# First loads, warmup and first attention step of a fused attention and gated-MLP kernel, re-ordered

## The chip, the cores and the metric

The kernel runs on one core of one Trainium2 chip. The metric is device time in microseconds (us), lower is better; each version is run several times and the median is quoted. "Faster" or "slower" needs a difference of 2%.

Engines are named PE (TensorE matmul), PEld (its weight loads), DVE (VectorE), ACT (ScalarE), POOL (GpSimd) and SP (SyncE); a "q" behind a name is that engine's instruction queue, where DMAs (memory transfers) are issued. "L133" is line 133 of the kernel in question; the same line of code has other numbers in other versions.

## The reference, cut to what matters

```python
x = A_x                                   # 1 x 2048 x 448, bf16
xn = _layernorm(x)
# A: 16 heads of 28, each query sees the 256 keys up to itself
q, k, v = split(xn @ wqkv)
p = softmax(where(0 <= i - j < 256, q k^T * 28**-0.5, -1e9))
A = (p @ v) @ wo
# B: gated MLP, hidden size 1792
B = (gelu(xn @ w_gate) * (xn @ w_up)) @ w_down
return x + A + B
```

x is cut into 16 tiles of 128 rows, the queries into four blocks of four tiles. The change concerns only what comes before and in the first step: loads of x and of the q, k, v weights, layer norm of tiles 0 to 7, their transposes, v of tiles 0 to 3, q and k of the first head group, and the first score groups. Below, this stretch of some 20 us is called the head.

## The kernel before

The loads. `wv` is the v part of the weights, `wraw` the q and k part; both queues, SP's and ACT's, share the same 16 DMA engines.

```python
nc.sync.dma_start(out=x_sb[:, 0, :], in_=xv[:, 0, :])
nc.scalar.dma_start(out=x_sb[:, 1, :], in_=xv[:, 1, :])
nc.sync.dma_start(out=x_sb[:, 2:4, :], in_=xv[:, 2:4, :])
nc.sync.dma_start(out=wv[:, 0:3, :], in_=rows(A_wqkv, 0, 3)[:, :, 2 * D:3 * D])
nc.scalar.dma_start(out=wraw[:, 0:3, :], in_=rows(A_wqkv, 0, 3)[:, :, 0:2 * D])
# ... the last 64 rows of wv and wraw, two small loads each
nc.sync.dma_start(out=x_sb[:, 4:8, :], in_=xv[:, 4:8, :])
# ... later x_sb[:, 8:16, :]
```

The first step. `stat` is a tile's mean and variance on DVE, `rstd` turns them into 1/sigma on ACT (the row of operations called `lnv` and `rstd_all`), `norm` writes the normalised tile `xn` in a wide and a narrow piece, `transp` transposes it on PE (`tp`) and copies it to `xnT`, `pads` spreads q,k columns into 32-wide heads (`wqp`, `wkp`), `gen_v` and `gen_qk` are the v, q and k products (`pv`, `pq`, `pk`).

```python
warmup(10)                     # matmuls on zeros, only to raise PE's clock
stat(0); rstd(0, 1); stat(1); rstd(1, 1)
norm(0); transp(0, 1, nc.scalar.copy, "o")
norm(1); warmup(1); transp(1, 1, nc.scalar.copy, "d")
stat(2); stat(3); rstd(2, 2)
# ... pads of the first head group, w3p (the last 64 rows of q and k)
norm(2); norm(3)
run(gen_v(0, (0,)))            # v of tiles 0, 1
qk = gen_qk(0, (0,), 0, 2 * P); next(qk)
transp(2, 1, nc.scalar.copy, "o"); transp(3, 1, nc.vector.tensor_copy, "m")
stat(4)
run(qk)                        # q, k of the first group, first half
stat(5)
pads(nc.vector.tensor_copy, wqp, slice(1, 4)); pads(nc.vector.tensor_copy, wkp, slice(1, 4))
run(gen_qk(0, (0,), 2 * P, 2 * P))   # second half
rstd(4, 2)
stat(6)
v23 = gen_v(0, (2,)); next(v23); next(v23)   # v of tiles 2, 3, ahead of the scores
norm(4); norm(5); stat(7)
```

## Time and profile before

The kernel before took 227.83 us (227.75 to 228.38, 3 runs).

| what, profiled execution of before | us |
|---|---|
| first matmul of v (`pv`) | 7.51 |
| first exp (`p_sb`) starts | 14.11 |
| fourth score group (`sc`) starts | 20.40 |
| first load of the gelu table on ACT | 39.45 |
| second load of the gelu table | 89.53 |
| last residual addition starts | 221.31 |
| span end | 226.5 |

The last four rows are landmarks: the two table loads stand at the end of the first and of the second query block. The profile's span is some 1.7 us shorter than the device time.

From the DMA issues of the first 13 us of the kernel before (what, queue, count, size, us from issue to landing):

```profile
x_sb<-in_A_x_dram SPq DMA_DIRECT2D x1, 448.0 KB, 4.5
...
x_sb<-in_A_x_dram SPq DMA_DIRECT2D x1, 224.0 KB, 3.6
```

The first line is x tiles 4 to 7: issued at 4.78, so landed at about 9.3. The second is x tiles 2 and 3: issued at 1.26, landed at about 4.86. And from the DMA view of the kernel before, 4 to 5 us only (total; then the ScalarE queue q10: packets, MB, share of the 16 engines' time):

```profile
DMA packets 255, 0.40 MB, mean 401 GB/s; under 512 B 15, under 2 KB 255, under 8 KB 255
...
q10 hardware_dynamic: 207, 0.37, 95.7%
```

Here, between 4 and 5 us, the early loads run at 401 GB/s, in packets of 1.8 KB (0.37 MB by 207).

### The profile page before, as it was taken

The numbers are of one execution on the slowest core, as the hardware profiler recorded it, in microseconds if no ns is written. First come the engines' busy times: TensorE is split into PE (matmuls) and PEld (weight loads), VectorE is DVE, ScalarE is ACT, GpSimd is POOL, SyncE is SP. The second block draws the span as 40 slices with busy tenths as digits, with TensorE's granted clock in tenths as the row PEclk, the third lists the DMA queues.
The fourth block names the chain that finished last, engine by engine and source line by source line (L and its number), as shares of the span: only waits on it lengthen the run. The fifth ranks groups of instructions, "written<-read, shape, count | busy, mean of one in ns | idle before, by whom it ended". The sixth has DMA issues, their size and how long they took to land.

```text
span 226.5 us, 5405 instructions
## 1 busy us (share of the span) xinstructions
PE 215.8 (95%) x2237; PEld 97.2 (43%) x2262; DVE 147.5 (65%) x353; ACT 133.2 (59%) x129; POOL 43.2 (19%) x63
## 2 busy tenths in 40 slices
PE   6989999999999999999999999999999999999990
PEld 2533333344444444444444445444344435334570
DVE  5896887778675637588655666596355776679310
ACT  4578897524878876423768886333576776763000
POOL 8514767320000002222000002222000002222000
PEclk9999999999999999999999999999999999999998
DMA  6914999111100100001300100000000000100011
GB/s 215 332 24 74 322 320 303 60 23 37 37 0 24 25 5 22 26 0 28 68 0 23 25 4 25 23 0 0 0 4 20 25 5 5 42 3 0 22 42 29
DMA packets 17990, 12.69 MB, mean 56 GB/s; under 512 B 9704, under 2 KB 16936, under 8 KB 17960
## 3 DMA queue, kind: packets, MB, share of 16 engines
q1 hardware_dynamic: 17416, 11.48, 18.3%
q10 hardware_dynamic: 544, 0.80, 1.0%
q8 instruction: 19, 0.31, 0.6%
q14 instruction: 11, 0.09, 0.1%
HBM read 8.77 MB, written 1.84 MB: 47 GB/s over the span
## 4 chain that ended last, share of the span: by engine, by line
PE 79%; DVE 6%; DMA 3%; SPq 3%; ACT 3%; POOL 2%; issue 2%; DVEq 0%
PE po L301 16%; PE gt L218 15%; PE u L218 11%; PE po L296 5%; PE sc L539 5%; PE gt L223 5%; PE ov L501 4%; PE ue L218 4%; PE pq L218 3%; PE pk L218 3%; PE pv L218 3%; DMA wraw<-in_A_wqkv_dram 2%; POOL oN L451 2%; PE pq L223 2%; DMA oc<-ri 1%
## 5 line engine op out<-in xcount | busy, mean ns | idle before, releaser
L543 ACT ACTIVATE p_sb<-sc 128x2048 bf16<-128x2048 f32 (+2 forms) x42 | 73.9, 1759 | 10.2 <-PE sc L539 8.5
L301 PE MATMUL po<-wd,hT 128*128 128x448 bf16 (+1 forms) x238 | 50.0, 342 | 0.0
L376 ACT ACTIVATE ge<-gt 128x1024 bf16<-128x1024 f32 x28 | 28.7, 1024 | 35.3 <-PE u L223 22.1
L218 PE MATMUL gt<-xnT,wg 128*128 128x512 bf16 x162 | 39.3, 380 | 1.2 <-issue 0.8
L451 POOL TENSOR_TENSOR oN<-oc,rb 128x512 bf16<-128x512 f32 x10 | 12.7, 1269 | 118.6 <-DVE rb L489 50.1
L380 DVE TENSOR_TENSOR hT<-ge,u 128x512 bf16<-128x512 bf16 x42 | 26.9, 682 | 11.7 <-ACT ge L376 11.5
L218 PE MATMUL u<-xnT,wu 128*128 128x512 bf16 x120 | 30.2, 379 | 0.3
L301 PEld LDWEIGHTS <-hT 128*128 128x128 bf16 x238 | 21.6, 98 | 18.6 <-issue 2.2
L432 DVE TENSOR_TENSOR p_sb<-p_sb,masks 128x256 bf16<-128x256 bf16 (+1 forms) x90 | 24.6, 328 | 0.0
L218 PEld LDWEIGHTS <-wg 128*128 128x128 bf16 x168 | 15.1, 98 | 22.1 <-issue 6.0
L218 PEld LDWEIGHTS <-wu 128*128 128x128 bf16 x168 | 16.0, 98 | 19.2 <-issue 1.0
L507 DVE TENSOR_TENSOR oc<-oc,ov 128x512 f32<-128x512 f32 x12 | 8.2, 687 | 19.4 <-ACT oc L506 19.4
L539 PE MATMUL sc<-qT,kT 32*64 32x320 bf16 (+7 forms) x640 | 16.9, 263 | 0.5 <-ACT p_sb L543 0.3
L442 POOL TENSOR_SCALAR_AFFINE_SELECT p_sb<-p_sb 128x512 bf16<-128x512 bf16 (+1 forms) x20 | 14.3, 732 | 13.2 <-ACT p_sb L543 13.2
L306 DVE TENSOR_TENSOR res<-po,x_sb 128x448 bf16<-128x448 f32 (+1 forms) x17 | 9.9, 585 | 10.3 <-PE po L301 9.9
L296 PE MATMUL po<-wo,oN 128*128 128x448 bf16 (+1 forms) x68 | 16.3, 343 | 0.0
L506 ACT COPY oc<-ov 128x512 f32<-128x512 f32 x12 | 7.0, 585 | 15.8 <-POOL oN L451 13.4
L267 DVE CAST kT<-pk 128x512 bf16<-128x512 f32 (+1 forms) x17 | 11.0, 649 | 7.9 <-PE pk L223 7.9
L451 POOL TENSOR_TENSOR oN<-oc,l 128x512 bf16<-128x512 f32 x6 | 8.4, 1394 | 30.6 <-DVE l L468 30.6
L335 DVE CAST hT<-ue 128x512 bf16<-128x512 f32 x14 | 9.0, 686 | 7.1 <-PE ue L223 7.1
L223 PE MATMUL gt<-xnT,wgu 64*128 64x512 bf16 x49 | 13.6, 380 | 0.1
L266 ACT CAST qT<-pq 128x512 bf16<-128x512 f32 (+1 forms) x17 | 9.5, 558 | 6.5 <-PE pk L223 6.5
(75 smaller groups left out, 239.9 us busy)
## 6 DMA issues: line engine op xcount, KB each, us to landing
out_dram<-res SPq DMA_DIRECT2D x15, 112.0 KB, 1.8
wd<-in_B_w_down_dram SPq DMA_DIRECT2D x1, 1568.0 KB, 12.6
wu<-in_B_w_up_dram SPq DMA_DIRECT2D x1, 1344.0 KB
wg<-in_B_w_gate_dram SPq DMA_DIRECT2D x1, 1344.0 KB, 10.7
x_sb<-in_A_x_dram SPq DMA_DIRECT2D x1, 896.0 KB, 5.7
wraw<-in_A_wqkv_dram ACTq DMA_DIRECT2D x1, 672.0 KB, 4.9
x_sb<-in_A_x_dram SPq DMA_DIRECT2D x1, 448.0 KB, 4.5
wo<-in_A_wo_dram SPq DMA_DIRECT2D x4, 98.0 KB
```

What stands on the lines that cost most here:

```text
L218: nc.tensor.matmul(ps, lhsT=lhs(c), rhs=rhs(c), start=start and c == 0, stop=stop and c == 2, skip_group_check=True)
L223: nc.tensor.matmul(ps, lhsT=lhs[p0:p0 + 64], rhs=rhs[p0:p0 + 64], start=start, stop=stop, tile_position=(p0, 0), skip_group_check=True)
L267: nc.vector.tensor_copy(out=kT[:, g, ts], in_=pk[:, 0:n])
L296: nc.tensor.matmul(po[:, 0:w], lhsT=oN[:, g, cs], rhs=wo[:, g, lo:up], start=(g == 0), stop=False, skip_group_check=True)
L301: nc.tensor.matmul(po[:, 0:w], lhsT=hT[:, f, cs], rhs=wd[:, f, lo:up], start=False, stop=(f == NF - 1), skip_group_check=True)
L376: nc.scalar.activation(out=ge[:, :, :], in_=pr["gt"][:, :, :], func=ACT.Gelu_apprx_tanh)
L380: nc.vector.tensor_tensor(out=hT[:, f + i, :], in0=ge[:, i, :], in1=u[:, :], op=ALU.mult)
L432: nc.vector.tensor_tensor(out=reg, in0=reg, in1=m, op=ALU.mult)
L442: nc.gpsimd.affine_select(out=reg, in_=reg, pattern=mid + [[1 if diag else -1, min(w, P)]], compare_op=ALU.is_ge, fill=0.0, base=0 if diag ...
L451: nc.gpsimd.tensor_tensor(out=oN[:, g, :], in0=oc[:, :], in1=inv, op=ALU.mult)
L539: nc.tensor.matmul(ss[k0:k0 + nk, j, col:col + nq], lhsT=kT[r, g, kt * P + k0:kt * P + k0 + nk], rhs=qT[r, g, qb * QB + q0:qb * QB + q0 + ...
L543: nc.scalar.activation(out=p_sb[:, :, 0:ncol], in_=ss[:, :, 0:ncol], func=ACT.Exp, scale=SCALE)
```

## The change

The intent is to start the first attention step sooner. The v weights and only those q,k columns that the first head group needs are loaded first; eight warmup matmuls instead of eleven stand ahead of the transposes; the first score group runs between the v products of tiles 2 and 3, so that exp starts before all of v is done; and statistics, norms and masks that are needed later move behind it. Two narrow norm pieces go to POOL.

```diff
+    wqk = rows(A_wqkv, 0, 3)[:, :, 0:2 * D]
-    nc.sync.dma_start(out=x_sb[:, 2:4, :], in_=xv[:, 2:4, :])
     nc.sync.dma_start(out=wv[:, 0:3, :], in_=rows(A_wqkv, 0, 3)[:, :, 2 * D:3 * D])
-    nc.scalar.dma_start(out=wraw[:, 0:3, :], in_=rows(A_wqkv, 0, 3)[:, :, 0:2 * D])
...  # last rows of wv
+    nc.sync.dma_start(out=x_sb[:, 2:4, :], in_=xv[:, 2:4, :])
+    for t in range(2):
+        nc.scalar.dma_start(out=wraw[:, 0:3, t * D:t * D + 4 * Dh], in_=wqk[:, :, t * D:t * D + 4 * Dh])
...  # last rows of wraw
+    for t in range(2):
+        nc.sync.dma_start(out=wraw[:, 0:3, t * D + 4 * Dh:(t + 1) * D], in_=wqk[:, :, t * D + 4 * Dh:(t + 1) * D])
     nc.sync.dma_start(out=x_sb[:, 4:8, :], in_=xv[:, 4:8, :])
...
-    make_masks()                      # now behind norm(3)
...
-        for eng, lo, n, src in ((nc.vector, 0, D, 0), (nc.vector, D, 64, 384)):
+        for eng, lo, n, src in ((nc.vector, 0, D, 0), (nc.gpsimd if t in (2, 3) else nc.vector, D, 64, 384)):
...
-    warmup(10)
+    warmup(8)
...
-    warmup(1)
...
-    stat(4)
     run(qk)
+    stat(4)
+    run(gen_qk(0, (0,), 2 * P, 2 * P))
     stat(5)
+    rstd(4, 2)
     pads(...); pads(...)
-    run(gen_qk(0, (0,), 2 * P, 2 * P))
-    rstd(4, 2)
-    stat(6)
-    v23 = gen_v(0, (2,))
+    v23 = gen_v(0, (2,), False)       # may be interrupted by the scores
     next(v23)
-    next(v23)
-    norm(4); norm(5); stat(7)
+    def ahead():                      # runs after the first exp
+        for t in (4, 5): norm(t); dma_transp(t)
+        stat(6); stat(7)
...
-            aux = [lambda: rstd(6, 2), lambda: (norm(6), norm(7), loads()), lambda: None] ...
+            aux = [ahead, lambda: rstd(6, 2), lambda: (norm(6), norm(7), loads())] ...
```

More of the change, by code (lines that the diff above doesn't have):

```diff
@@ L233, in bank, with gen_v @@
         return psum.tile([P, QB], f32, name=name, tag=tag, bufs=2 if tag == "m" else 1)
-    def gen_v(qb, ts):
+    def gen_v(qb, ts, hold=HOLD):
         for t in ts:
@@ L244, in gen_v @@
                 pvs.append(pv)
-                yield (570, HOLD) if i else 570
+                yield (570, hold) if i else 570
             for i in range(2):
@@ L617 @@
     norm(3)
+    make_masks()
     run(gen_v(0, (0,)))
@@ L622 @@
     transp(3, 1, nc.vector.tensor_copy, "m")
+    run(qk)
     stat(4)
-    run(qk)
+    run(gen_qk(0, (0,), 2 * P, 2 * P))
     stat(5)
+    rstd(4, 2)
     pads(nc.vector.tensor_copy, wqp, slice(1, 4))
     pads(nc.vector.tensor_copy, wkp, slice(1, 4))
-    run(gen_qk(0, (0,), 2 * P, 2 * P))
-    rstd(4, 2)
-    stat(6)
-    v23 = gen_v(0, (2,))
+    v23 = gen_v(0, (2,), False)
     next(v23)
-    next(v23)
-    norm(4)
-    norm(5)
-    stat(7)
+    def ahead():
+        for t in (4, 5):
+            norm(t)
+            dma_transp(t)
+        stat(6)
+        stat(7)
     def loads():
-        for t in range(4, 8):
+        for t in (6, 7):
             dma_transp(t)
@@ L655 @@
         if qb < 2:
-            aux = [lambda: rstd(6, 2), lambda: (norm(6), norm(7), loads()), lambda: None] * (1 - qb) + [lambda t=t: stat(t) for t in range(8, 12)] * (1 - qb) + [lambda: rstd(4 * qb + 8, 4)]
+            aux = [ahead, lambda: rstd(6, 2), lambda: (norm(6), norm(7), loads())] * (1 - qb) + [lambda t=t: stat(t) for t in range(8, 12)] * (1 - qb) + [lambda: rstd(4 * qb + 8, 4)]
         if qb == 0:
@@ L660 @@
             feeds = [Feed((v23, 360), (gen_qk(0, (1, 2, 3)), 3 * QK1), (gen_proj(1), PROJ), (gen_up(0, early), UP1 * len(early)))]
-            feeds[0].held = True
         else:
```

## The prediction

> **What bounds the kernel now.** I read the page's totals and slices first, then the chain of work that ended last, cut to the first 45 us and in order of time, then the timeline of the first 42 us.
>
> ```profile
> PE 215.8 (95%) x2237; PEld 97.2 (43%) x2262; DVE 147.5 (65%) x353; ACT 133.2 (59%) x129; POOL 43.2 (19%) x63
> ...
> PE   6989999999999999999999999999999999999990
> ```
>
> TensorE (PE) is busy 95% of the span. Each slice is 5.66 us; only the first, second and last are not full. The change touches nothing after the first slices, so it can only win what is lost before PE becomes the bound. The chain says where that is:
>
> ```profile
> 4.14 4.17 DMA wraw<-in_A_wqkv_dram
> 8.30 0.02 issue
> 8.32 0.28 DVE w3p L614
> 8.61 1.06 DVE xn L199 x4
> ...
> 15.83 0.19 DVE mv_all L186
> 16.02 0.02 issue
> 16.05 0.30 ACT lnv L190
> 16.35 0.02 issue
> 16.37 0.20 ACT rstd_all L191
> 16.58 0.47 ACT qT L266
> 17.05 1.36 ACT p_sb L543
> 18.41 0.04 issue
> 18.45 0.29 PE sc L539 x4
> ```
>
> Columns: start, length, what. Until 8.3 us the chain is a weight load (the last rows of q and k), then VectorE (DVE) without a gap until 16.0, then ScalarE (ACT), and from 18.45 on it is PE back to back, to the end of this view. So the quantity to predict is how much earlier the third score group (18.45) and what follows it start. The timeline gives the anchors:
>
> ```profile
> 1.96 4.45 PE L180 MATMUL wps<-wo 128*128 128x512 bf16 x10 [1.96 <-DVE wo L160]
> ...
> 6.20 0.63 PE L213 MATMUL tp<-ident,xn 128*128 128x128 bf16 x4
> ...
> 7.51 1.31 PE L218 MATMUL pv<-wv,xnT 128*128 128x448 bf16 x6 [0.23 <-ACT xnT L214]
> ...
> 8.32 0.28 DVE L614 COPY w3p<-wraw 128x448 bf16<-128x448 bf16 x1 [0.57 <-DMA wraw<-in_A_wqkv_dram]
> ```
>
> The transposes stand behind the tenth warmup matmul; w3p cost DVE 0.57 us of waiting. Later:
>
> ```profile
> 14.11 1.88 ACT L543 ACTIVATE p_sb<-sc 128x2048 bf16<-128x2048 f32 x1
> ...
> 16.05 0.34 PE L539 MATMUL sc<-qT,kT 32*128 32x384 bf16 x4 [0.34 <-ACT p_sb L543]
> ```
>
> The first exp starts at 14.11 and the second score group waits for it (one score buffer).
>
> **What the Trainium skill says.** "TensorE: Matmul & The Clock Gate", The HAM clock gate: PE runs at half rate until about 3.4 us of sustained work have filled a free-running window; 427 ns for 512 columns cold, 216 warm. The trace agrees: warmups start 0.43 us apart, up to 6.62, and the 448-column matmuls from 7.51 are 0.19 apart. "DMA: Bandwidth & Descriptors", Specifications: line rate needs pieces of at least 512 B. The new q,k loads have rows of 4 heads x 28 x 2 B = 224 B; no early load of the kernel before is that small, so no line shows the price. Same page, Queues, rings and completion order: each DMA engine takes turns between the queues; here in 3 to 4 us the SyncE queue used 56% and the ScalarE queue 41%, so both advance together. "SBUF — State Buffer", Who interferes with whom: DVE in its two-port modes and GpSimd (POOL) exclude each other. The trace fits: four norm instructions took 1.09 us at 14.18 with POOL idle and 1.42 us at 17.03 beside POOL selects.
>
> **The change, part by part.** I follow the compiled order and waits of the changed program with durations from the rows of before; all times are us from the span's start.
>
> *Warmup 10 to 8, the eleventh gone.* The eight end at 1.96 + 8 x 0.427 = 5.37. The norm of tile 0 ends about 5.35 (started 4.78), so the transposes start at 5.37, not 6.20. ACT's copy followed them by 0.67 (6.20 to 6.87) and takes 0.585: xnT ready at 6.63, first v matmul 6.67 instead of 7.51. The six matmuls and two halves keep their 1.6: done 8.27 (9.11).
>
> *Loads.* Before the end of x tiles 2,3 now lie x 0,1 (224 KB), wv (448), q,k columns (168) and themselves (224): 1064 KB = 1.09 MB. At the 333 GB/s of 2.0 to 6.2 us (windows view), from 2.2, that is 5.5, plus some 0.5 to be reported: 6.0. They landed at 4.86 before (1.26 + 3.6), but DVE had no time for them before 5.98. So an estimated loss of 0.1: statistics of 2 and 3 run 6.1 to 7.6. wv lands near 5, ahead of 6.67 (before: 1.72 + 5.7 = 7.42, just in time). The last q,k rows land near 6.3 (112 KB more) and w3p no longer waits: 7.85 to 8.13 instead of 8.32.
>
> *Norms.* rstd of 2,3 is ready at 8.14, DVE does only the two wide norms (2 x 0.33, until 8.85; before 9.67 for all four pieces) and POOL the two narrow ones. ACT: wkp pad to 8.6, v_sb to 9.15 (9.67). It frees the bank for the tile 3 transposes at 9.2; copy out 9.66 to 10.08 (10.57); first k half product and kT cast 10.24 to 10.64; stat 4 to 11.4; second kT cast 11.4 to 11.8 (13.51). The second cast gains 1.7, because stat 5 and both wide pads (0.75 + 0.88) now follow it.
>
> *Scores between the v tiles.* The three matmuls of v tile 2 fit in 11.28 to 11.85; scores start at 11.9 (13.58), those of tile 3 follow. Exp would start at 12.43, but ACT now has rstd of 4,5 just ahead, needing stat 5: 11.8 to 12.58, then 0.30 + 0.20 with gaps: exp 1 starts **13.1** against 14.11, ends 14.97. The gain shrinks from 1.7 to 1.0 here.
>
> *Behind exp 1.* v_sb of tile 2 now stands behind exp on ACT (to 15.45), but the next k product needs the bank of tile 3, which DVE frees at 14.0 after the wide pads (to 13.4). So k runs 14.05 to 14.7, scores 2 at 15.1 (16.05). ACT: v_sb 0.5, qT 0.5, exp 2 15.9 to 17.35; scores 3 at 17.4 instead of 18.45. The rstd of 6,7 moved behind exp 2, so ACT then does 0.5 of that, qT to 18.4, exp 3 to 19.35. PE waits for that qT, its k product starts 18.45 (19.33) and scores 4 at **19.5** against 20.40. From there instruction orders are identical and PE is the bound.
>
> *Sum.* 20.40 - 19.53 = 0.87 us. Nearly all of it is the 0.83 by which the transposes start earlier (6.20 - 5.37), carried through; the pauses of PE further on change place more than size. I take off a little for the small-row loads and POOL below: **0.8 us**, 227.83 - 0.8 = 227.0.
>
> **The rivals.** (1) *Loads take the win back.* If 224 B rows cost as much as 512 B rows, the 168 KB weigh like 384 and x tiles 2,3 land 0.6 later, at about 6.6; the whole chain from stat 2 moves by 0.5: gain 0.3, time 227.5. For: line rate was used up (DMA busy share 1.00 in 2.0 to 6.2). Against: the two queues share, and q,k come after x 1 on theirs. (2) *The clock stays low longer.* The window is free-running; in this execution it switched near 6.6[...]. If it switches at 8, the v matmuls from 6.67 take 0.7 longer, where before their cold part was covered by DVE; gain 0.2 to 0.4, time 227.5. Against: PE still works without a pause over 0.3 until 8.2. (3) *POOL in DVE's way.* The masks (0.76 + 4.97 of POOL) move from 3.5-9.3 to about 9-14.8, beside DVE's pads and norms. If these lengthen by 30% as seen at 17.03, v_sb of tile 3 ends 0.4 later and scores 2 come at 15.5; but scores 3 wait for exp 2 anyway, so little is lost: 227.2. (4) *Late transposes.* norm 6,7 fall about 0.5 later (18.95 against 18.45) while their consumer comes 0.87 earlier. The last transpose landed near 22.1 for a use at 23.8; now about 22.5 for 22.9. If it slips by 0.8, PE waits 0.4: 227.4.
>
> **Range and chances.** The mechanism is certain in direction up to 12 us, the four rivals each take 0.1 to 0.6 and seldom all. The best case, with exp 1 at 12.9 and no DMA loss, is about 226.4; two rivals together give 227.8. Repeats of before differ by 0.6. So 226.3 to 227.8. 2% is 4.6 us, nearly the whole of the eleven warmups (4.45 + 0.43) and five times the sum above; faster 1%, slower 1%, within 98%.
>
> **What will show it.** Right: transposes at 5.4, first v matmul near 6.7, no DMA wait before w3p, exp 1 near 13.1 after rstd (not after a PE wait), scores 4 near 19.5, and the same PE lengths after. Wrong: a DMA wait before stat 2 of over 0.4, v matmuls more than 0.3 apart, the first k product after scores 1 waiting for ACT's v_sb, or a DMA wait before the v tiles 6,7. A gain above 1.2 us would mean that rstd of 4,5 does not hold up exp 1; a loss would mean that one of the moved ACT items costs more than 0.9 us on PE.

## The result, and the profile after

The changed kernel took **227.88 us** (227.77 to 227.95, 4 runs), the kernel before in the same rounds 227.79 us (227.65 to 228.38, 4 runs). The ratio is 0.9999, 95% interval 0.9981 to 1.0017: the same. (Ratios here are the mean time of one kernel's runs over that of the other's in the same rounds, so not quite the ratio of the medians quoted.) "Within 2%", which the prediction gave 98%, came true. But the predicted gain of 0.8 us is not there, and 227.88 lies 0.08 above the predicted range.

From the page of the changed kernel, the totals and PE's 40 slices:

```profile
PE 217.7 (96%) x2259; PEld 96.2 (43%) x2259; DVE 147.9 (65%) x351; ACT 133.0 (59%) x129; POOL 44.5 (20%) x65
...
PE   6899999999999999999999999999999999999991
```

PE is full from the third slice on (before, the third slice had an 8). The chain of work that ended last, first 45 us in order of time (start, length, what):

```profile
1.25 3.83 DMA wraw<-in_A_wqkv_dram
...
6.05 5.71 DMA x_sb<-in_A_x_dram
11.78 0.64 DVE st L188
...
13.72 0.30 ACT lnv L193
14.25 1.76 ACT p_sb L546
...
16.93 1.36 ACT p_sb L546
18.33 0.29 PE sc L542 x4
```

Before, a DVE sequence set the pace from 8.3 to 16.0 us. Now, in this execution, loads set it up to 11.78: SP could issue x tiles 4 to 7 only at 6.05 (4.78 before), behind the remaining q,k columns, and they took 5.71 us instead of 4.5. The timeline of the first 21 us gives the steps that the prediction had put numbers on:

```profile
5.34 1.17 PE L216 MATMUL tp<-ident,xn 128*128 128x128 bf16 x8
...
6.48 0.63 DVE L188 BATCH_NORM_STATS2 st<-x_sb 128x6 f32<-128x448 bf16 x1 [0.34 <-DMA x_sb<-in_A_x_dram]
...
6.66 1.31 PE L221 MATMUL pv<-wv,xnT 128*128 128x448 bf16 x6
...
8.72 1.25 POOL L202 TENSOR_SCALAR xn<-x_sb,mv_all,rstd_all 128x64 bf16<-128x64 bf16 x2 [5.08 <-ACT rstd_all L194]
...
10.30 0.43 DVE L217 COPY xnT<-tp 128x512 bf16<-128x512 bf16 x1 [0.41 <-PE tp L216]
...
11.78 0.63 DVE L188 BATCH_NORM_STATS2 st<-x_sb 128x6 f32<-128x448 bf16 x1 [0.48 <-DMA x_sb<-in_A_x_dram]
...
14.16 1.86 ACT L546 ACTIVATE p_sb<-sc 128x2048 bf16<-128x2048 f32 x1
...
20.28 0.40 PE L542 MATMUL sc<-qT,kT 32*128 32x128 bf16 x8
```

The transposes and the first v product are as early as intended (0.86 and 0.85 us ahead of before). The lead then melts: 0.34 us of waiting for x tiles 2,3, the POOL pieces, 0.48 us of waiting for x tile 4. The first exp is at 14.16, where it was at 14.11, and the fourth score group is 0.12 us earlier than before. The table loads are at 39.33 and 89.13 and the last addition at 221.01.

The transfers, in the same two views as before, first the issues of the first 13 us of the changed kernel:

```profile
x_sb<-in_A_x_dram SPq DMA_DIRECT2D x1, 448.0 KB, 5.7
...
x_sb<-in_A_x_dram SPq DMA_DIRECT2D x1, 224.0 KB, 3.5
```

then 4 to 5 us of the changed kernel:

```profile
DMA packets 833, 0.29 MB, mean 294 GB/s; under 512 B 649, under 2 KB 833, under 8 KB 833
...
q10 hardware_dynamic: 607, 0.13, 59.3%
```

The DMA engines are as occupied as before but move 0.29 MB instead of 0.40. A small packet of q10 costs 59.3% of 16 engines for 1 us over 607 packets, 15.6 ns for about 214 B, that is 14 B/ns; before it was 95.7% over 207, 74 ns for about 1.8 KB, 24 B/ns. By this estimate, the 168 KB of early q,k columns weigh like 290 KB. The 224 B rows are not the whole of it: the other queue now carries rows of 896 B (v, x) where q10 had 1.8 KB rows before, and e8, which has no row under 512 B among its early loads, also moved only 290 GB/s in 4 to 5 us, in 356 packets of about 0.8 KB at 47 ns each.

### The profile page after: what moved, and what is told of

The parts are those of the page before. It is cut to its first block, busy times and chain, and to the rows that moved or that the text cites. A ratio compares the mean times of both kernels' runs of the same rounds, so it can differ in the third digit from the quotient of the medians.

```text
span 226.0 us, 5430 instructions
## 1 busy us (share of the span) xinstructions
PE 217.7 (96%) x2259; PEld 96.2 (43%) x2259; DVE 147.9 (65%) x351; ACT 133.0 (59%) x129; POOL 44.5 (20%) x65
## 3 DMA queue, kind: packets, MB, share of 16 engines
HBM read 8.77 MB, written 1.84 MB: 47 GB/s over the span
## 4 chain that ended last, share of the span: by engine, by line
PE 80%; DMA 6%; ACT 4%; DVE 3%; SPq 2%; POOL 2%; issue 1%; ACTq 0%; DVEq 0%
PE po L304 16%; PE gt L221 16%; PE u L221 11%; PE po L299 5%; PE sc L542 5%; PE gt L226 5%; PE ue L221 4%; PE ov L504 4%; PE pq L221 3%; PE pv L221 3%; PE pk L221 3%; DMA x_sb<-in_A_x_dram 3%; ACT p_sb L546 2%; DMA wraw<-in_A_wqkv_dram 2%; POOL oN L454 2%; PE pq L226 2%
## 5 line engine op out<-in xcount | busy, mean ns | idle before, releaser
L221 PE MATMUL gt<-xnT,wg 128*128 128x512 bf16 x168 | 40.5, 380 | 0.1
L509 ACT COPY oc<-ov 128x512 f32<-128x512 f32 x12 | 7.0, 585 | 15.6 <-POOL oN L454 10.7
L221 PE MATMUL pq<-xnT,wqp 128*128 128x512 bf16 (+1 forms) x51 | 13.2, 368 | 0.0
```

The costliest lines, as they stand in the source:

```text
L221: nc.tensor.matmul(ps, lhsT=lhs(c), rhs=rhs(c), start=start and c == 0, stop=stop and c == 2, skip_group_check=True)
```

## The experiments

Twelve kernels ran, in four batches; the kernels of one batch ran on one chip and share the runs of the kernel before (11 in each batch; medians, e1 to e4, e5 to e8, e9 to e11, e12: 227.99, 227.73, 228.38 and 228.50 us). Those medians differ by 0.8 us, so a time is only compared with before in its own batch. Differences of a few tenths cannot be read from the times; for those the landmarks of the profiled runs serve. But each profile is one execution. Where two profiles have the same instructions up to the first table load, that load differs by 0.06 us (before and e5), 0.21 (e3 and e6) and 0.52 (changed and e7, see there); smaller differences between two profiles show nothing yet.

| kernel | first exp | table load 1 | load 1 to load 2 | wait near 85 us | load 2 to last addition | last addition to end |
|---|---|---|---|---|---|---|
| before | 14.11 | 39.45 | 50.08 | 2.10 | 131.78 | 5.2 |
| changed | 14.16 | 39.33 | 49.80 | 1.83 | 131.88 | 5.0 |
| e1 | 13.73 | 39.11 | 50.06 | 2.08 | 131.78 | 5.2 |
| e2 | 15.52 | 40.96 | 50.12 | 2.16 | 131.88 | 4.8 |
| e3 | 13.37 | 38.72 | 50.31 | 2.33 | 131.81 | 5.5 |
| e4 | 13.99 | 39.16 | 49.82 | 1.84 | 131.88 | 5.5 |
| e9 | 13.39 | 38.72 | 49.80 | 1.82 | 131.79 | 5.2 |
| e10 | 13.26 | 38.72 | 49.87 | 1.90 | 131.77 | 5.3 |
| e11 | 14.46 | 40.21 | 50.12 | 2.14 | 131.88 | 5.7 |
| e12 | 15.12 | 40.49 | 49.88 | 1.91 | 131.80 | 5.6 |

In the expectations, "theory L" is that the loads take the gain back, its rival that the shorter warmup carries the gain; "D" is that a head gain is real and is given back later. Each kernel differs in one part from the one named with it, except e8 (two); the order part of e9 is a bundle.

### e1: the warmup alone

```diff
 # on the kernel before
-    warmup(10)
+    warmup(8)
...
-    warmup(1)
```

> The kernel before with eight warmups and no eleventh, nothing else. Theory L (the loads decide the head): the transposes start at 5.4, but the v weights still land near 7.4, so the first v matmul stays at 7.5 and the first exp at 14.1: time unchanged within 0.2 us. Rival W (the warmups were what held the head): first v matmul near 6.7, scores 4 up to 0.8 us earlier than 20.40, time down by 0.5 to 0.8.

Measured: 227.85 us (227.37 to 228.55), ratio 0.9993 (0.9961 to 1.0025). The transposes came at 5.34, but the first v product only at 7.19: the v weights, issued at 1.72, landed 5.4 us later (5.7 in before). The first table load was 0.34 us earlier than before. The 0.86 us by which the transposes come earlier are thus worth at most 0.34, between the two expectations. They may be worth less: e5, which keeps the eleven warmups, happened to run its first ten in 3.70 us instead of 4.45, so that its transposes came at 5.49. Its v product then waited 1.04 us for the weights, to 7.46, and its first table load was at 39.39, 0.06 before that of the kernel before.

### e2: the new load order alone

The load lines of the diff above, on the kernel before, nothing else.

> The kernel before with the new order of loads, nothing else. Theory L: x tiles 4 to 7 land near 11.8 instead of 9.3, while the statistics of tile 4 want them at 10.5; VectorE waits 1.0 to 1.3 us for a DMA, the first exp moves from 14.1 to 15.1 or later, time up by 0.7 to 1.2. Rival (the loads as such are harmless, POOL's slow narrow norms cost the gain): no DMA wait of over 0.3 us, time unchanged or down by 0.2.

Measured: 229.09 us (228.37 to 229.51), ratio 1.0034 (1.0002 to 1.0066). The first table load is 1.51 us later than before. From the timeline of this run, the statistics of tile 4:

```profile
11.98 0.63 DVE L189 BATCH_NORM_STATS2 st<-x_sb 128x6 f32<-128x448 bf16 x1 [1.35 <-DMA x_sb<-in_A_x_dram]
```

With the order of before, DVE asks for x tile 4 at 10.63 and stands idle for 1.35 us. The new loads alone cost time: theory L holds.

### e3: the changed kernel with the old loads

```diff
 # on the changed kernel: the load lines put back as before
```

> The changed kernel with the loads of before in their old order, everything else of the change kept. Theory L: no DMA wait before the statistics of tile 4; the first v matmul is back at 7.5 and w3p at 8.3, yet the first exp starts near 13.4 and scores 4 near 19.8, time down by 0.4 to 0.7 against before. Rival (POOL's narrow norms and the rstd ahead of the first exp cost the gain): first exp stays at 14.0 or later, time as before within 0.2.

Measured: 228.06 us (227.16 to 229.05, 6 runs), ratio 1.0001 (0.9972 to 1.003). The timeline of this run:

```profile
7.33 1.30 PE L217 MATMUL pv<-wv,xnT 128*128 128x448 bf16 x6 [0.61 <-DMA wv<-in_A_wqkv_dram]
...
13.37 1.86 ACT L542 ACTIVATE p_sb<-sc 128x2048 bf16<-128x2048 f32 x1
```

The v product now waits for its weights and starts 0.67 us later than in the changed kernel, and yet the first exp starts 0.79 us earlier, since no statistic waits for x. A second pair agrees in sign: e6 repeats the head of e3 and e7 that of the changed kernel, and their first exps are at 13.17 and 13.64, the first table loads at 38.51 and 38.81. The fourth score group is at 19.49, where the prediction had 19.5. So in the head the predicted gain exists (0.73 us at the first table load) and the new loads take back 0.3 (e6 against e7) to 0.6 us (e3 against the changed kernel) at the first table load. In the time, however, it was not to be seen in this batch.

### e4: x tiles 4 to 7 ahead of the remaining q,k columns

```diff
+    nc.sync.dma_start(out=x_sb[:, 4:8, :], in_=xv[:, 4:8, :])
     for t in range(2):
         nc.sync.dma_start(out=wraw[:, 0:3, t * D + 4 * Dh:(t + 1) * D], ...)
-    nc.sync.dma_start(out=x_sb[:, 4:8, :], in_=xv[:, 4:8, :])
```

> The changed kernel with one line moved: x tiles 4 to 7 are issued ahead of the remaining q and k columns. Theory L: they land before 11.2, VectorE's wait of 0.48 us at 11.8 is gone, the first exp starts near 13.6 instead of 14.16, scores 4 near 19.8 instead of 20.28, time down by 0.4 to 0.6. Rival (something else, POOL or ACT, sets the first exp): wait gone but first exp still at 14.0 to 14.2, time as before.

Measured: 227.97 us (227.42 to 228.30, 6 runs), ratio 0.9993 (0.997 to 1.0016). The wait before tile 4 is gone (statistics at 11.52), but x tiles 2,3 now came later (6.79, a wait of 0.75 us). The first table load is 0.17 before that of the changed kernel, less than two executions of the same head differ (e7). In this execution, what one tile won in the shared transfers another lost.

### e5 to e8: the wait near 85 us

In e3 the lead was 0.61 us over the changed kernel at the first table load and 0.10 at the second. In between, in the second query block, DVE waits for the last of four 2 KB transfers (`oc<-ri`) before it can spread the softmax sums (`rb<-oc`), and an exp and PE's gate product stand behind that. In e5 to e7 these transfers are issued one step earlier; e8 does it with another load order, in which the whole q,k block stands on SP's queue behind the v weights and x tiles 2,3.

```diff
-            if qb and i in (6, 8):
+            if qb and i in (5, 8):       # back(): reciprocal and the four transfers
```

```diff
 # e8, besides: x0, wv, x2:4 and then, on the same queue
+    nc.sync.dma_start(out=wraw[:, 0:3, :], in_=rows(A_wqkv, 0, 3)[:, :, 0:2 * D])
```

e5, on the kernel before:

> The kernel before with one number changed: in the second to fourth query block the inverse sums of head group 0 are sent back by DMA one step earlier (after step 5 instead of 6). Theory G (a head gain is given back near 85 us, where VectorE waits 2.1 us for that DMA, POOL's product and ScalarE's copy follow it, and the last exp and the first gate matmul follow that): the wait before the shuffle at 85.0 disappears or falls under 0.5 us, PE's 0.3 us before the gate matmul goes too, the second gelu table load comes 0.3 to 0.5 us earlier, time down by 0.2 to 0.5. Rival (that wait bounds nothing): the wait goes, the table load and the time stay within 0.1.

e6, on e3:

> The changed kernel with the old loads and the earlier send-back. Theory G: the head gain of 0.7 us seen at the first gelu table load (38.7 against 39.45) is still there at the second (near 88.5 against 89.5) and at the last residual add (220.3 against 221.3); time 0.7 to 1.0 below before. Rival: another point takes it back, the last residual add comes at 220.8 or later.

e7, on the changed kernel:

> The changed kernel with the earlier send-back alone. Theory L with G: its head is only 0.1 us ahead (39.33 against 39.45) because of the late x tiles, so with the wait gone it ends like the kernel before with the same edit, within 0.2 us. Rival (the changed kernel holds a gain that only this wait hides): it beats that one by 0.5 or more.

e8, on the changed kernel with the single queue:

> As the old loads with the earlier send-back, but the whole q and k block goes on the same queue behind x tiles 2, 3 and the v weights, in rows of 1792 B. Theory L: v weights land near 5 and no load before 11 us is late by over 0.4 us, the first v matmul comes at 6.7; first exp near 13.2, last residual add 220.2, time 0.8 to 1.1 below before. Rival: on one queue the q and k block comes too late, VectorE waits over 0.7 us for it, first exp at 13.7 or later.

Measured: e5 228.14 us (227.64 to 228.76), ratio 1.0017 (0.9998 to 1.0035); e6 229.05 (227.91 to 229.52), 1.0054 (1.003 to 1.0078); e7 228.09 (227.59 to 228.64), 1.0012 (0.9993 to 1.0031); e8 230.92 (229.47 to 231.99), 1.0152 (1.0125 to 1.0178); 6 runs each. The idea failed. In e5 the second table load did move 1.38 us ahead (88.15), but only ACT's load: PE now waited 0.72 us at 78.27 for DVE's copy of the sums (`oc`), DVE 0.93 us for the sums' transfer at 85.30, and PE's gate product behind it stands at 89.89, in before at 89.56. In e8 DVE waited 1.12 us, to 8.71, for the q,k block, and the first exp came at 14.71, as its rival said. The profiled execution of e6 has its last addition at 220.63, 0.68 before that of the kernel before, but its runs are slower than before; what the slower ones lost is in no kept trace.

e7 shows more, since up to the first table load it is the changed kernel. From its chain and its timeline:

```profile
3.00 3.42 DMA x_sb<-in_A_x_dram
...
8.69 1.26 POOL xn L202 x2
```

```profile
11.18 0.62 DVE L188 BATCH_NORM_STATS2 st<-x_sb 128x6 f32<-128x448 bf16 x1
...
13.64 1.86 ACT L546 ACTIVATE p_sb<-sc 128x2048 bf16<-128x2048 f32 x1
```

In this execution x tiles 4 to 7, issued at 6.08, landed after 4.7 us (5.71 in the changed kernel's profile), and DVE did not wait for them. The chain runs through x tiles 2,3 and the two norm pieces on POOL instead, the first exp comes at 13.64 and the first table load at 38.81. So the wait before tile 4 belongs to some executions of the changed kernel and not to all. Against e5, which has the same second-block edit, e7 is 0.58 us ahead at the first table load and 0.40 at the last addition (221.04 and 221.44), more than its expectation had; yet both profiles end at 226.7, and the medians are equal to 0.05 us.

### e9 and e10: the order alone; and a filled gap

e9 is the kernel before with its own loads and eleven warmups, and only the order part of the change (scores between the v tiles, norms and statistics re-timed, narrow norms on POOL, masks later). e10 is e3 with

```diff
     transp(1, 1, nc.scalar.copy, "d")
+    warmup(3)
```

> The kernel before with its own loads and its own eleven warmup matmuls; only the order part of the change (first step's scores between the two v tiles, norms and statistics re-timed, two narrow norms on POOL, masks later). Theory D (each head gain is real and is given back later, at the wait near 85 us and at the end): transposes at 6.2 and first v matmul near 7.5 as before, no DMA wait before the statistics of tile 4, first exp near 13.6, fourth score group near 19.9, first gelu table load near 39.0 (before 39.45), second near 89.2, span end 226.2 to 226.7, ratio 0.998 to 1.001. Theory C (the loose times of the old-loads kernels come from PE standing idle in front of the v tiles while the clock rises): here PE has no idle stretch there over 0.3, so the runs lie within 0.8 us of each other and the median is 227.3 to 227.6. Rival (the order part is worth nothing at the head): first exp 14.0 to 14.2, first table load 39.3 to 39.5.

> The order part with the loads of before and eight warmup matmuls, and three more warmup matmuls behind the transposes of tile 1, where PE stood idle for 0.6 us waiting for the v weights. Theory C (idle PE while the clock rises makes the run times loose and eats the head gain): first v matmul 7.3 to 7.5, first exp 13.4 to 13.6, and the runs now lie within 0.8 us of each other with a median of 227.2 to 227.5. Theory D (gain given back later; spread from the transfers' landing times): head as with C, first table load near 38.8, but the runs still lie 1.2 us or more apart, median 227.7 to 228.1, span end 226.0 to 226.8.

Measured: e9 227.55 us (227.22 to 227.79, 6 runs) beside before's 228.38 (227.45 to 228.90, 11 runs), ratio 0.9978 (0.9956 to 0.9999). e10 227.57 us (227.38 to 228.81, 6 runs), ratio 0.9997 (0.9968 to 1.0026). Both have the first table load at 38.72, as e3 has. The chain of e9, 4 to 22 us:

```profile
1.72 5.61 DMA wv<-in_A_wqkv_dram
...
7.38 1.30 PE pv L217 x6
...
13.80 0.59 PE pq L217 x2
...
20.64 2.44 DMA xnT<-xn
```

In e9 the v product starts at 7.38, only 0.13 us earlier than before, and still the fourth score group is at 19.51, 0.89 us earlier. (Its transposes came at 5.71 and not at the expected 6.2, since ten warmups took 3.92 us here; but the v product had to wait for its weights in any case, 0.84 us.) The order part alone gives the whole predicted head gain; the shorter warmup adds nothing to it (e3, with both, has the same 38.72). Which piece of the order part gives it was not separated. PE decides from 13.8 to 17.6, then DVE with the norms of tiles 6,7 (1.87 us from 18.19; before, 1.42 us from 17.03); what stops all three kernels at 38.72 is in the last line: a transposing DMA of x tiles 6,7 that lands at 23.08, for which a v product waits (0.25 us longer than before in e9).

Theory C, that PE's idle stretch makes run times loose, fell: of the three, e9 has the longest such stretch (0.84 us) and the tightest runs (0.57 us apart), e10 has none over 0.3 and spreads over 1.43 us.

The wait near 85 us, in the kernel before:

```profile
85.01 0.01 DVE L489 LOAD_MASK_SELECT rb<-oc  x1 [2.10 <-DMA oc<-ri]
```

and in e9:

```profile
84.01 0.01 DVE L488 LOAD_MASK_SELECT rb<-oc  x1 [1.82 <-DMA oc<-ri]
```

In the table above, the time from load 1 to load 2 less this wait is 47.96 to 47.98 us in all ten profiles. So whatever an execution waits there, 1.82 to 2.33 us, it takes the whole program with it, and the value goes with the version only in part: the three kernels with the order of before waited 2.08 to 2.16, and those with the new order 1.82 to 1.91, but for e3 (2.33) and e11 (2.14). e3, e9 and e10 reach the first table load at the same time and waited 2.33, 1.82 and 1.90. That is what ate e3's lead. The last stretch differs too, 4.8 to 5.7 us, in which the profile shows nothing but the last output store. Between these ten profiles the two together differ by more than the whole gain in question.

### e11: two warmups

```diff
 # on the changed kernel
-    warmup(8)
+    warmup(2)
```

> The changed kernel with two warmup matmuls instead of eight: a test of the prediction's rival 2 (the clock stays low longer). If PE's clock needs the warmups, the v matmuls from about 6.7 stand 0.37 apart instead of 0.19, the two v tiles take over 2 us instead of 1.3, and all up to the fourth score group is 0.3 to 0.8 later than in the changed kernel (20.28), time 228.1 to 228.7. If the clock rises without them (transposes and v matmuls suffice, or the window falls well), the transposes start as early as the norm allows, near 5.3, and all stands as in the changed kernel to 0.15 us, time 227.7 to 228.0.

Measured: 228.97 us (228.48 to 229.63, 4 runs), ratio 1.0031 (1.0004 to 1.0059). The v product in this run:

```profile
6.36 2.42 PE L221 MATMUL pv<-wv,xnT 128*128 128x448 bf16 x6
```

Six matmuls in 2.42 us instead of 1.31: PE was still at its low rate. (The granted clock in the profile reads 1.00 here, as it does in the other runs, so this rate is read from the length of the matmuls.) The fourth score group is 0.31 us later than in the changed kernel (20.59; against e7's 19.76, 0.83 later), and a wait of 0.49 us for a late transpose behind it brings the first table load to 0.88 later. So eight warmups are needed at least in part. With eight, PE was at its full rate in time in the profiles of the changed kernel and of e7 (each of the six matmuls lasted 0.35 to 0.36 us), while in e4 and e12, also with eight, the longest of the six still lasted 0.56 and 0.55 us. The prediction's second rival is real in kind; it did not strike in the two profiles of the changed head, and was worth some 0.2 us of one matmul in those two others.

### e12: the q,k block in one piece again

```diff
 # on the changed kernel
-    for t in range(2):
-        nc.scalar.dma_start(out=wraw[:, 0:3, t * D:t * D + 4 * Dh], ...)
+    nc.scalar.dma_start(out=wraw[:, 0:3, :], in_=wqk)
...
-    for t in range(2):
-        nc.sync.dma_start(out=wraw[:, 0:3, t * D + 4 * Dh:(t + 1) * D], ...)
```

> The changed kernel with its v weights first and x tiles 2,3 behind them, but with the q,k block loaded whole on the ScalarE queue as before (no 224 B rows, no second q,k load ahead of x tiles 4 to 7). This tells apart why x tiles 4 to 7 land late in the changed kernel (11.76). Theory L1 (the split is to blame: small rows lower the rate and the rest of q,k stands ahead of x tiles 4 to 7): x tiles 4 to 7 land near 9.3 as before, no DMA wait before the statistics of tile 4; v matmuls at 6.7; statistics of tile 2 at 6.3 to 6.8; first exp 13.2 to 13.5, fourth score group near 19.4, first table load 38.5 to 38.8, median 227.3 to 227.7. Rival L2 (v weights ahead of x is what hurts): statistics of tile 2 after 7.0 with a DMA wait over 1.0, x tiles 4 to 7 after 11, first exp 14.0 or later, median 227.8 to 228.3.

Measured: 229.68 us (229.14 to 231.23, 6 runs), ratio 1.0064 (1.0033 to 1.0096). The timeline, statistics of tiles 2 and 4:

```profile
7.92 0.63 DVE L185 BATCH_NORM_STATS2 st<-x_sb 128x6 f32<-128x448 bf16 x1 [1.80 <-DMA x_sb<-in_A_x_dram]
...
12.66 0.62 DVE L185 BATCH_NORM_STATS2 st<-x_sb 128x6 f32<-128x448 bf16 x1
```

and its DMA view of 4 to 5 us:

```profile
DMA packets 289, 0.39 MB, mean 392 GB/s; under 512 B 9, under 2 KB 289, under 8 KB 289
```

Each theory is half right. As L1 said, without the split the small packets are gone, the rate is back at 392 GB/s, and x tiles 4 to 7 are issued at 4.78 and land 4.5 us later (about 9.3), so tile 4 waits for nothing. But as L2 said, the whole q,k block then runs beside the v weights and x tiles 2,3 come at 7.92, 1.44 us later than in the changed kernel, and that costs more. The split was there for a reason: it saves tiles 2,3 and hands the delay to tiles 4 to 7. The kernel before had x tiles 2,3 first and the v weights at 7.4; they were not on its chain, but they head the chains of e3, e5 and e9.

## Why the prediction was right or wrong

- **The page of before**: misread in one place that changes nothing. The slices that are not full are the first, the third (8) and the last; the second has a 9.
- **Transposes and first v product**: right to 0.03 us (5.34 and 6.66). PE was at its full rate, w3p waited for no transfer.
- **X tiles 2,3**: too optimistic by 0.38 us (6.48 instead of 6.1; 6.45 in e7). The term that was mis-sized is the rate: the prediction divided its 1.09 MB by the 333 GB/s that the kernel before moved in 2.0 to 6.2 us. The windows view gives 279 for the changed kernel there; all five profiled kernels with the split rows have 277 to 282, the eight with the q,k block whole on ACT's queue 333 to 346. With 279 the same sum comes to 6.6. This was rival 1, which the prediction named, with small rows weighing like 290 KB instead of the rival's 384. How much of it is row size and how much the emptier ACT queue is not separated: e8, with large rows and nearly all on one queue, has 271.
- **Narrow norms on POOL**: it was given as a relief for DVE and their cost was not worked out. The two pieces took 1.25 us on POOL, 0.65 each, where DVE takes 0.29 for such a piece (groups by shape, kernel before), and PE's transposes waited for them. The copy of tile 3 came at 10.30 instead of 9.66, of which 0.26 us is beyond the lateness of the tiles (0.25 in e7, where the two pieces stand on the chain). That all of it is POOL's is argued, not shown: no run had the order part with these norms on DVE.
- **Statistics of tile 4**: the failed step, with the two above. "stat 4 to 11.4" assumed without saying so that x tiles 4 to 7 are in memory by then. The prediction followed the delay of tiles 2,3 through the reordered queue and stopped there. In the profile of the changed kernel they landed at 11.76 instead of about 9.3, and 0.48 us of waiting stood on the path. The sum of these three, 0.38 + 0.26 + about 0.42, is the 1.06 us by which exp 1 (14.16) missed 13.1. With the same loads the wait was 1.35 us in e2, while in e7 (landed at about 10.8) and e11 (about 11.2) there was none; in e7 the first two steps alone make exp 1 miss by 0.54. That the new loads cost time is shown by e2 and by the pairs of e3. How much is the later issue (6.05 instead of 4.78) and how much the small packets is not separated: e12 took both away at once, and e4, with the small packets but the tiles issued at 5.05, only shows that no wait was left at 11.52.
- **Exp 1 behind rstd of tiles 4,5, not behind a PE wait**: right.
- **"Nearly all of it is the 0.83 by which the transposes start earlier, carried through"**: wrong. e1 finds at most 0.34 for it alone, e5 next to nothing, and next to the order part it adds nothing (e3 against e9, both 38.72), since with the old loads the v product waits for its weights. e9 shows that the order part alone gives 0.89 at the fourth score group. The number 0.87 came out for a kernel with the old loads, but for another reason than the one given; that is luck.
- **POOL masks in DVE's way** (rival 3): hardly seen for the masks; the four norms at 14.97 took 1.20 us beside the masks, against the 1.09 us with POOL idle that the prediction quotes.
- **Late transposes** (rival 4): true. The norms of tiles 6,7 were to end at 18.95; they started then, took 1.89 us beside POOL's selects on `p_sb`, and ended at 20.84 (20.06 in e9). PE lost 0.06 us by it in the changed kernel, which had little lead, and 0.25 in e9.
- **"From there PE is the bound"**: true on the average, but with one exception that the page's 95% hides: the wait for a 2 KB transfer near 85 us passes to the end in full. It differs by up to 0.5 us between profiles, so that one needs several runs to see anything of a gain of 0.7 us.
- **The range**: its top, 227.8, rested on "two rivals together". Rival 1 struck at tiles 2,3, in some executions again at tile 4, and POOL's pieces came on top. "Within 2%" was a safe call: none of the twelve experiments moved the time by more than 1.6%.

So where did the 0.8 us go? In the two profiled executions of the changed head 0.12 and 0.64 us of lead over before were left at the first table load; x tiles 2,3, the POOL pieces and, in one of them, tile 4 took the rest. What was left is of the size of what the wait near 85 us and the last stretch differ by, and the medians show none of it (227.88 against 227.79; e7 against e5 228.09 against 228.14).

What stays open: why e3, e6 and e10 spread over 1.4 to 1.9 us while e9 does not (before's own 11 runs in e9's batch spread over 1.45, so e9's may be chance), why the same loads land up to 1 us apart, and why the 2 KB transfer takes longer in some executions. A 16 KB instruction packet passes the DMA engines within the 81 to 85 us of these profiles; that it is the cause is only a guess.

Of the versions that ran, e9 is the best: 0.22% under before by the ratio, an interval that just excludes no gain, and one of twelve such intervals. By the 2% rule it is still "the same". It did not run beside the changed kernel, so that it beats it (227.55 against 227.88 in other rounds) is likely, not shown.

## What to carry to other kernels

When loads already run at the full rate, moving one ahead means moving others back: list for every tile behind it when it will land and when it is first read, not only for the next one. Splitting a load to get its urgent part sooner can cost twice, by the small rows and by what the rest then delays. Look at a second execution of the same code before you name a wait as the cause: here tile 4 waited 0.48 us in one and not at all in the other. And before crediting a gain to the first thing that moves, ask what the instruction at the end of the chain was waiting for: here it was the order of DVE's and PE's work, and reordering alone, without touching the loads, kept the gain in the head.

## What the Trainium skill lacked or had wrong

- "DMA: Bandwidth & Descriptors", Specifications, gives 512 B as the least size for line rate; the page has no measured time for rows of 224 B on the queues of SP and ACT. Its section Why small descriptors are slow (HBM only) has a fixed overhead of about 3 cycles per packet beside one cycle per 32 B. An estimate from that is 1.4 times the cost per byte of 1792 B rows for 224 B rows. Measured here, beside a second queue: 15.6 ns per packet of about 214 B (14 B/ns) against 74 ns per packet of 1.8 KB (24 B/ns), so 1.8 times. Packets of 0.8 KB, above the 512 B, took 47 ns in e8 (17 B/ns).
- "GPSIMD Engine Reference", 3.1 Elementwise — side-by-side cycle accounting, compares the engines at 2048 elements a row (GPSIMD 1.96 times slower than DVE). Here pieces of 64 elements in bf16 took 0.65 us each on POOL and 0.29 on DVE. That is 2.2 times, near the page's ratio; the section has no row for so small a piece.
- No page has it that a transfer of 2 KB between two places in SBUF, at the same place of the program, is waited for between 1.82 and 2.33 us from one profiled execution to another (ten profiles of ten versions), and that this is passed on one to one (47.96 to 47.98 us for the rest of the stretch).
